# Linear attention and two MoE layers on one core: keys in groups of two token tiles, and a planner that stays with one kind of product

## The chip, the cores and the metric

One Trainium2 chip; the kernel runs on one of its NeuronCores. The metric is the device time of one execution in microseconds, as a median of several executions. TensorE (PE) multiplies, VectorE (DVE) and ScalarE (ACT) do elementwise work and reductions, GpSimd (POOL) reduces over partitions, and the queue of SyncE (SP) issues most DMA transfers. Products land in PSUM, which has eight banks; everything else that an engine reads stands in SBUF, 128 partitions wide.

## The reference

```python
# q, k, v: (4 batches, 8 heads, 576 tokens, 64), float32; w_phi: (64, 128)
def phi(x):
    proj = einsum('bhsd,df->bhsf', x, w_phi)
    proj = proj - max(abs(proj), axis=-1, keepdims=True)
    return concatenate([exp(proj), exp(-proj)], axis=-1)

q_p, k_p = phi(q), phi(k)
kv = einsum('bhsf,bhsd->bhfd', k_p, v)
z = sum(k_p, axis=2)
x = einsum('bhsf,bhfd->bhsd', q_p, kv) / (einsum('bhsf,bhf->bhs', q_p, z)[..., None] + 1e-6)
x = x.transpose(0, 2, 1, 3).reshape(2304, 512)         # tokens x (heads * 64)
h = x @ moe_w_in;  x = maximum(0.01 * h, h) @ moe_w_out      # 512 -> 2048 -> 512
h = x @ moe2_w_in; r = maximum(h, 0); out = (r * r) @ moe2_w_out
```

## The kernel before

Three stages follow each other on TensorE: the attention of batch 0; layer 1 with the attention of batches 1 to 3 put between its products; layer 2.

**Kinds of product.** A number that must keep float32 accuracy is multiplied either plain (TensorE takes such a product in two passes, which the trace shows as two records) or split into two halves that float32r holds exactly, with three float32r products in place of one (high by high, low by high, high by low). The copy that makes the high half is a CAST or an ACTIVATE, the low half a TENSOR_TENSOR on VectorE.

**Attention** (`k_pair` and `q_pair`) goes by batch and pair of heads, 16 pairs in all. The 576 keys of a head are four tiles of 128 tokens and 64 left-over tokens; the left-over tokens of both heads make a fifth tile, with a load of its own (krt). Per tile, in this order: `proj` multiplies the keys by w_phi into a PSUM bank (split from batch 1 on, but plain for the left-over tokens of all batches), `center` takes the maximum on VectorE (kmx, L1128) and negates it (L1130), `expo` runs two exponentials per head on ScalarE straight from the bank (kp, L1142), which then is free, and `kv` multiplies them by the values (vt, plain products of 65 columns) into an accumulating bank. For batches 1 to 3 a key tile can use bank 1 only, a query product bank 1 or 0, and bank 0 is also the accumulator's: two banks serve all the attention there. `q_pair` does half of the queries of a pair: product, copy out of the bank (qps), an absolute maximum over partitions on GpSimd (qm), exponentials, numerator and denominator products (with kvh, which is kv, or from batch 2 on its halves kvh and kvl), two copies per head out of the bank (qnum, qden), a reciprocal of 1.9 us on VectorE (L1321), a product, and the two halves of x, written to xr.

**Layer 1** (`moe`) goes over five blocks of tokens and 16 chunks of d_ff, 80 steps. A step of a full block is twelve products of 512 columns with xr and weights (called x products below) and twelve with gh and gl, the halves of the activation. A block can begin when the x of all its tokens is written; block 0 needs all of batch 0. **Layer 2** (`h_unit`, `y_unit`) uses products of 384 columns from xc and of 256 columns from its weights.

**SBUF.** arena, room and more hold the weights of layer 1 in slots; later arena, room, w and w_2 hold those of layer 2. Slots of arena begin at varied offsets of 32 bytes (`LINE`), and `new` pads some tiles and shifts others by 32 bytes.

**Order.** Nothing waits by hand. `Plan.add` records each operation with the engines that may run it, a cost, a position (its priority, built from the numbers in `P`) and what it reads and writes; `Plan.order` plays all engines forward and gives each the ready operation of lowest position, and the instructions are issued in that order. An operation with two possible engines (most high halves, some copies) goes to the one that takes it first. Each engine then works through its own queue in order. While TensorE has nothing in the planner's first 95 us, it is given filler products on zeros (`fill`).

Of the kernel before, what the change touches and what calls it, by code (L numbers as in the profile page):

```python
# [41 lines left out]
LINE = 16  # L42
SHIFTED = ("kvh", "kvl", "gh", "gl")
MOVED = ("gh", "gl")

P = dict(
    ring=6, wf=2, raws=3, k0=-115.69, kz=(-22.16, -25.13, -28.64), kp0=14.6, kp=22.44, ks=1.84, kvd=6.19, kb=0, pk=0, pq=0, pn=1, qk=2.73, qk2=13.5,
    q20=-8.75, qd=(3.27, -21.24, 20.79, 10.82, -2.12, -17.72, 26.78), wlead=30.91, wl0=-7.1, ydelay=16.3, xs=(174.51, 74.74, 10.17), xl=11.4, xk=4.78,
    xk2=8.22, xst=74.82, xld=24.14, lead=43.44, slead=-24.15, w2lead=29.72, ylead=53.84, evac=-12.29, stage0=-99.0, stage=14.29, stage2=-10.59,
    pl=-1.44, c_alt=43.95, sq_alt=7.93, klead=27.27, qlead=25.53, hi_alt=0.31, dve_alt=34.87, port=1.25, lat=0.28, issue=0.47, dma=2.5, rate=320e3,  # L50
    kvc=0.9, fill=95, cold=4.98, coldf=2.2,
# [29 lines left out]
class Plan:  # L81
# [31 lines left out]
    def order(self, filler=None):  # L113
        now, n_done, seq, port = 0.0, 0, 0, 0.0
# [6 lines left out]

        def make_ready(op):
            for e, (_, extra) in op.engines.items():
                heapq.heappush(ready[e], (op.pos + extra, id_of[op], op))
# [19 lines left out]
        while n_done < len(self.ops):  # L144
            for e in free:
                while free[e] <= now:
                    skipped, found = [], None
                    while ready[e]:
# [4 lines left out]
                        if can(op):  # L153
                            found = op
# [29 lines left out]
                    if e == "PE" and now < P["cold"]:  # L184
                        cost *= P["coldf"]
# [32 lines left out]
def attention_moe_moe(ctx: ExitStack, tc: tile.TileContext, qd, kd, krd, vd, wpd, wd, out):  # L218
# [30 lines left out]
    arena = ring.tile([128, NSLOT * size], F32, name="arena")  # L249
    more = first.tile([128, 2, chunk], F32, name="more")  # L250
    first.tile([128, LINE // 2], F32, name="edge")
    inside = [(k, 0) for k in range(RING - 2)] + [(k, 1) for k in range(RING)]
    slots = [[None, None] for _ in range(RING)]
    starts, words = [], 0
    for k, h in inside:
        words += LINE // 2 if h == 0 else LINE // 2 * (words // (LINE // 2) % 2)
        starts.append(words)
        slots[k][h] = arena[:, words:words + chunk]
        words += chunk
# [51 lines left out]
    def new(tag, shape, dtype, shift=0):  # L311
# [4 lines left out]
        for d in shape[1:]:  # L316
            size *= d
# [48 lines left out]
    def pe(c):  # L366
        return {"PE": (c, 0)}
# [1088 lines left out]
```

## Time and profile before

| | us |
|---|---|
| median of 3 executions | 988.54 (987.70 to 989.52) |
| profiled execution, its time | 989.24 |
| profiled execution, its span | 987.2 |
| TensorE busy in the span | 963.8 (98%) |
| VectorE busy | 784.7 (79%) |
| ScalarE busy | 562.2 (57%) |
| GpSimd busy | 90.6 (9%) |

The span runs from the first to the last instruction of the profiled execution; times within it count from its start. Layer 1 begins at 72.6 us, the attention ends at about 476 us, layer 2 begins at some 610 us. The granted clock of TensorE was 0.997 of full speed over the whole span. Matmuls are pipelined: a product's length in a row overlaps the next one's, so how long a run of products takes is read from the start of the run to the start of the next row.

### The profile page before, as it was taken

To read this page: it belongs to the slowest core of one execution; us is meant where nothing else is said; L and a number is where in the kernel's file an instruction comes from. 1 tells how busy PE (TensorE), PEld (TensorE's weight loads), DVE (VectorE), ACT (ScalarE), POOL (GpSimd) and SP (SyncE) were. 2 spreads that over 40 slices of the span, in tenths; PEclk is the share of its full clock that TensorE was granted. 3 is DMA by queue.
4 is the path that set the end of the run, shared out by engine and by line. 5 is a ranking of instruction groups with operands and counts; after the bars stand their busy time and mean duration, and the time that the engine had idled before them with its cause. 6 is when DMAs were issued, how large, how long until landed. Compare 5 with 4: busy or idle time off the path is not lost.

```text
span 987.2 us, 16603 instructions
## 1 busy us (share of the span) xinstructions
PE 963.8 (98%) x5855; PEld 859.7 (87%) x5855; DVE 784.7 (79%) x1678; ACT 562.2 (57%) x1325; POOL 90.6 (9%) x52
## 2 busy tenths in 40 slices
PE   9999999999999999999999999999999999999997
PEld 7788777878888788878888899999999999999996
DVE  6999999799999999996334421778997787888878
ACT  7988777777777887775333332343633434334342
POOL 2221011011110111010000000000000000200101
PEclk9999999999999999999999999999999999999999
DMA  7449889868988598991689489788975293918623
GB/s 268 148 170 290 293 288 317 276 240 280 313 302 292 192 319 280 330 321 64 226 304 339 171 295 333 314 341 281 301 293 207 114 361 146 275 20 306 153 76 64
DMA packets 90290, 244.37 MB, mean 248 GB/s; under 512 B 8032, under 2 KB 33504, under 8 KB 87136
## 3 DMA queue, kind: packets, MB, share of 16 engines
q1 hardware_dynamic: 86896, 239.12, 69.0%
q0 software_dynamic: 3312, 4.20, 2.9%
q8 instruction: 46, 0.75, 0.3%
q14 instruction: 36, 0.29, 0.1%
HBM read 166.48 MB, written 76.81 MB: 246 GB/s over the span
## 4 chain that ended last, share of the span: by engine, by line
PE 58%; DVE 32%; DMA 4%; issue 3%; ACT 2%; DVEq 0%; ACTq 0%; SPq 0%
PE bank L330 58%; DVE qden L1321 4%; DMA raw<-wd 3%; DVE wf L465 2%; DVE s L339 2%; DVE gl L339 2%; DVE room L339 2%; DVE kmx L1128 2%; DVE raw L460 2%; DVE g L970 1%; DVE qel L339 1%; DVE qm L339 1%; DVE qs L339 1%; DVE kmx L1130 1%; DVE qnum L1324 1%
## 5 line engine op out<-in xcount | busy, mean ns | idle before, releaser
L330 PE MATMUL bank<-gh,arena 128*128 128x512 f32 (+1 forms) x640 | 203.3, 376 | 0.0
L330 PE MATMUL bank<-xr,arena 128*128 128x512 f32 (+1 forms) x720 | 165.8, 374 | 0.0
L339 DVE TENSOR_TENSOR gl<-g,gh 128x512 fp32r<-128x512 f32 (+2 forms) x176 | 94.1, 539 | 68.6 <-ACT gh L334 68.1
L330 PEld LDWEIGHTS bank<-xr,arena 128*128 128x128 f32 x720 | 123.5, 188 | 22.2
L330 PEld LDWEIGHTS bank<-gh,arena 128*128 128x128 f32 x640 | 117.6, 189 | 20.0
L330 PE MATMUL bank<-gl,arena 128*128 128x512 f32 (+1 forms) x320 | 119.4, 373 | 0.3 <-DVE gl L339 0.3
L1251 POOL PARTITION_ALL_REDUCE qm<-qps x32 | 73.8, 2305 | 388.1 <-ACT qps L334 244.1
L334 ACT ACTIVATE gh<-g 128x512 fp32r<-128x512 f32 (+2 forms) x168 | 83.6, 502 | 36.9 <-PE bank L330 34.8
L1142 ACT ACTIVATE kp<-bank,kmx 128x128 f32<-128x128 f32 x288 | 82.3, 371 | 28.9 <-DVE kmx L1130 25.0
L625 ACT ACTIVATE g<-bank 128x512 f32<-128x512 f32 (+1 forms) x80 | 44.1, 552 | 82.0 <-PE bank L330 81.1
L330 PE MATMUL bank<-xc,w 128*128 128x384 f32 x504 | 89.8, 335 | 0.1
L330 PEld LDWEIGHTS bank<-xc,w 128*128 128x128 f32 x504 | 87.1, 188 | 0.6 <-DVE g L814 0.5
L330 PE MATMUL bank<-arena,sc 128*128 128x256 f32 x648 | 85.1, 283 | 0.1
L330 PEld LDWEIGHTS bank<-arena,sc 128*128 128x128 f32 x648 | 80.4, 188 | 1.8 <-DVE y L970 0.3
L334 ACT ACTIVATE sc<-s 128x512 fp32r<-128x512 f32 (+1 forms) x70 | 37.8, 541 | 73.8 <-DVE s L339 36.1
L330 PEld LDWEIGHTS bank<-vt,kp 128*128 128x128 f32 x576 | 71.4, 191 | 5.3 <-issue 1.5
L330 PE MATMUL bank<-vt,kp 128*128 128x65 f32 (+1 forms) x576 | 72.6, 271 | 0.6 <-ACT qnum L334 0.6
L330 PEld LDWEIGHTS bank<-gl,arena 128*128 128x128 f32 x320 | 60.5, 189 | 9.5 <-DVE gl L339 1.3
L339 DVE TENSOR_TENSOR sc<-s,sc 128x512 fp32r<-128x512 f32 (+1 forms) x96 | 51.6, 555 | 19.3 <-ACT sc L334 18.4
L814 DVE TENSOR_TENSOR g<-bank,g 128x384 f32<-128x384 f32 x72 | 40.0, 555 | 30.8 <-PE bank L330 24.9
L1321 DVE RECIPROCAL qden<-qden 128x288 f32<-128x288 f32 x32 | 62.2, 1944 | 0.8 <-ACT qden L1307 0.8
L330 PE MATMUL bank<-arena,gh 128*128 128x256 f32 x324 | 59.9, 281 | 0.0
(142 smaller groups left out, 1837.2 us busy)
## 6 DMA issues: line engine op xcount, KB each, us to landing
arena<-wsd SPq DMA_DIRECT2D x72, 512.0 KB, 5.2
raw<-wd SPq DMA_DIRECT2D x64, 512.0 KB, 5.0
xc<-xcd SPq DMA_DIRECT2D x28, 768.0 KB, 12.5
arena<-wcd SPq DMA_DIRECT2D x10, 1792.0 KB, 8.0
wsd<-arena SPq DMA_DIRECT2D x28, 512.0 KB, 5.7
wid<-room SPq DMA_DIRECT2D x24, 512.0 KB, 4.2
wcd<-room SPq DMA_DIRECT2D x24, 512.0 KB, 4.9
xcd<-xc SPq DMA_DIRECT2D x14, 768.0 KB, 10.1
```

The costliest lines, as they stand in the source:

```text
L330: nc.tensor.matmul(out=o, lhsT=lhsT, rhs=rhs, start=start, stop=stop, **kw)
L334: nc.scalar.activation(out=out, in_=in_, func=ACTF.Copy)
L339: ENG[e].tensor_tensor(out=out, in0=a, in1=b, op=ALU.subtract)
L460: nc.vector.tensor_scalar(out=low, in0=low, scalar1=29, scalar2=None, op0=ALU.logical_shift_right)
L465: nc.vector.scalar_tensor_tensor(out=t["f"].bitcast(I32), in0=high, scalar=3, in1=low, op0=ALU.logical_shift_left, op1=ALU.bitwise_or)
L625: nc.scalar.activation(out=t["g"], in_=banks[hb.bank][:, 0:N], func=ACTF.Prelu, alpha=0.01)
L814: nc.vector.tensor_tensor(out=t[o], in0=m(z), in1=t["a"], op=ALU.add)
L970: nc.vector.tensor_tensor(out=o, in0=a, in1=b, op=op)
L1128: nc.vector.tensor_reduce(out=mx[1], in_=o, axis=AX.X, op=ALU.max, apply_absolute_value=True)
L1142: nc.scalar.activation(out=u["kp"][:, s, h, :], in_=banks[pr.bank][:, h * 128:(h + 1) * 128], func=ACTF.Exp, scale=sg, bias=u["mx"][:, s, ...
L1251: nc.gpsimd.partition_all_reduce(out_ap=t["m"].rearrange("p h s -> p (h s)"), in_ap=t["ps"].rearrange("p h s -> p (h s)"), channels=128, r ...
L1321: nc.vector.reciprocal(out=t["d"], in_=t["d"])
```

## The change

What changes:

- Keys. `KGROUPS` names the groups. Batch 0 keeps five. In batches 1 to 3 the groups are left-over tokens with tile 0, tiles 1 and 2, and tile 3: 3, 4 and 2 heads' tiles with one maximum, one negation and one bank each. The left-over tokens come with the other keys in one load of 640 columns, and in batches 1 to 3 they are split with them and multiplied by the halves w2h and w2l.
- Planner. A product of layer 1 has the kind "m", all others none. If the ready product of lowest position on TensorE is of another kind than the last one, and one of the last kind is ready within `stick` = 2.0 of its position, that goes first; a change to "m" costs `switch` = 0.096 in the plan.
- Numbers. Nearly every position and several costs in `P` differ.
- Places. `LINE` shifts are gone. Slots of arena follow each other without gaps; for layer 2 the weights for y start 32 words (`STEP`) into arena, and other tiles are padded.
- Buffers. vt has one in place of two, kvh and kvl two in place of three, kmx four of another shape; kp is twice as long.
- Dead branches for `kb` are gone.
- Filler products go from 183 to 220.

```diff
-LINE = 16
-SHIFTED = ("kvh", "kvl", "gh", "gl")
-MOVED = ("gh", "gl")
+LINE = 8
+STEP = 32
+EDGE = 24
+KGROUPS = (
+    tuple(((t,), k) for k, t in enumerate((4, 0, 1, 2, 3))),
+    (((4, 0), 0), ((1, 2), 2), ((3,), 4)),
+)
...
-    ring=6, wf=2, raws=3, k0=-115.69, kz=(-22.16, -25.13, -28.64), kp0=14.6, kp=22.44, ks=1.84, kvd=6.19, kb=0, pk=0, pq=0, pn=1, qk=2.73, qk2=13.5,
+    ring=6, wf=2, raws=3, k0=-140.1, kz=(-10.15, -15.45, -39.25), kp0=13.19, kp=13.3, ks=2.06, kvd=6.19, kb=0, pk=0, pq=0, pn=1, qk=2.72, qk2=13.71,
...
+                    if e == "PE" and found and kind_of(found) != kind:
+                        rest = [i for i in ready[e] if i[2].engine is None and i[0] <= item0 + P["stick"] and kind_of(i[2]) == kind and can(i[2])]
+                        if rest:
+                            heapq.heappush(ready[e], (item0, id_of[found], found))
+                            item = min(rest)
+                            ready[e].remove(item)
+                            heapq.heapify(ready[e])
+                            found = item[2]
...
+                        if op.engines[e][2] and op.engines[e][2] != kind:
+                            cost += P["switch"]
+                        kind = op.engines[e][2]
...
-        "kt": ("a", 2), "krt": ("a", 2), "vt": ("a", 2), "kh": ("a", 1), "kl": ("a", 1), "kmx": ("a", 3), "ksb": ("a", 1),
-        "kp": ("a", 2), "kvf": ("a", 1), "kvh": ("a", 3), "kvl": ("a", 3),
+        "kt": ("a", 2), "vt": ("a", 1), "kh": ("a", 1), "kl": ("a", 1), "kmx": ("a", 3), "ksb": ("a", 1),
+        "kp": ("a", 2), "kvf": ("a", 1), "kvh": ("a", 2), "kvl": ("a", 2),
...
+    wslots = [arena[:, k * size + STEP * (k > 0):(k + 1) * size + STEP * (k > 0)] for k in range(NSLOT)] + [room, None, None, None]
+    shared = [arena[:, 0:size], arena[:, STEP:size + STEP]]
...
-        load(32768, tpos[0] - lead, get_r, w=[krt])
-        load(262144, tpos[0] - lead, get_k, w=[kt])
+        load(327680, tpos[0] - lead, get_k, w=[kt])
...
-        for n, (tt, pos) in enumerate(zip((4, 0, 1, 2, 3), tpos)):
-            m = 1 if tt == 4 else 2
+        for tiles, pos in KGROUPS[b > 0]:
+            pos = tpos[0] + P["ks"] * pos
+            heads = [(tt, h) for tt in tiles for h in range(1 if tt == 4 else 2)]
+            m = len(heads)
```

What this does to the order shows at three places. First TensorE in batch 1, between products of layer 1 (xr, gh and gl; room,kh and room,kl are split key products, vt,kp the products with the values, qs and qe query products and numerators; bank_75 and bank_76 are banks 0 and 1). Before:

```order
L330 MATMUL bank_76<-room,kh 128x256
L330 MATMUL bank_76<-room,kl 128x256
L330 MATMUL bank_76<-room,kh 128x256
L330 MATMUL bank_75<-vt,kp 128x65 x4
L330 MATMUL bank_81<-gh,arena 128x512
L330 MATMUL bank_81<-gl,arena 128x512
L330 MATMUL bank_81<-gh,arena 128x512
L330 MATMUL bank_82<-gh,arena 128x512
L330 MATMUL bank_82<-gl,arena 128x512
L330 MATMUL bank_82<-gh,arena 128x512
L330 MATMUL bank_77<-xr,arena 128x512 x6
L330 MATMUL bank_76<-room,kh 128x256
```

and in the new order:

```order
L343 MATMUL bank_76<-qs,arena 128x288 x2
L343 MATMUL bank_77<-xr,arena 128x512 x6
L343 MATMUL bank_76<-qe,kvh 128x288 x2
L343 MATMUL bank_75<-qe,kvh 128x288 x2
L343 MATMUL bank_77<-xr,arena 128x512 x6
L343 MATMUL bank_76<-room,kh 128x256
L343 MATMUL bank_76<-room,kl 128x256
L343 MATMUL bank_76<-room,kh 128x256 x2
L343 MATMUL bank_76<-room,kl 128x256
L343 MATMUL bank_76<-room,kh 128x256
L343 MATMUL bank_75<-qs,arena 128x288 x2
L343 MATMUL bank_79<-gh,arena 128x512
```

Before, one tile's three key products stand between stretches of layer 1 and the next tile's come behind twelve products of it; now two tiles' six products follow each other, and two numerators and a query product stand directly beside other attention products.

Second VectorE some 25 instructions ahead of the last write of batch 0's x (xr<-qnum and xr<-qnum,xr write x; raw<-raw, wf<-raw, arena<-wf and arena<-wf,arena shift, join, cast and split weights; qm<-qps,qm is the absolute maximum of a query product). Before:

```order
L336 CAST xr<-qnum 128x64
L339 TENSOR_TENSOR xr<-qnum,xr 128x224
L339 TENSOR_TENSOR xr<-qnum,xr 128x64
L465 SCALAR_TENSOR_TENSOR wf<-raw 128x512
L460 TENSOR_SCALAR raw<-raw 128x512
L339 TENSOR_TENSOR qm<-qps,qm 128x576
L1321 RECIPROCAL qden<-qden 128x288
L1324 TENSOR_TENSOR qnum<-qnum,qden 128x288
L1128 TENSOR_REDUCE kmx<-bank_76 128x2
L1130 TENSOR_SCALAR kmx<-kmx 128x2
L336 CAST xr<-qnum 128x32
L339 TENSOR_TENSOR xr<-qnum,xr 128x32
```

and in the new order:

```order
L473 TENSOR_SCALAR raw<-raw 128x512
L352 TENSOR_TENSOR xr<-qnum,xr 128x224
L352 TENSOR_TENSOR xr<-qnum,xr 128x64
L478 SCALAR_TENSOR_TENSOR wf<-raw 128x512
L352 TENSOR_TENSOR qm<-qps,qm 128x576
L349 CAST arena<-wf 128x512
L352 TENSOR_TENSOR arena<-wf,arena 128x512
L1143 TENSOR_REDUCE kmx<-bank_76 128x4
L1144 TENSOR_SCALAR kmx<-kmx 128x4
L1325 RECIPROCAL qden<-qden 128x288
L1328 TENSOR_TENSOR qnum<-qnum,qden 128x288
L473 TENSOR_SCALAR raw<-raw 128x512
```

Behind the same two writes of x (224 and 64 columns) the next reciprocal stood fourth; it now stands seventh, behind the cast and the split of a weight tile and a key group's maximum and negation.

Third SP's queue at the program's start (vt are values, kt keys, qt queries, raw weights). Before:

```order
L1080 DMA krt<-krd 64x128
L1076 DMA kt<-kd 128x512
L1084 DMA vt<-vd 128x650
L1212 DMA qt<-qd 128x576 x2
L1080 DMA krt<-krd 64x128
L1076 DMA kt<-kd 128x512
L1084 DMA vt<-vd 128x650
L1080 DMA krt<-krd 64x128
L444 DMA raw<-wd 128x512
L1212 DMA qt<-qd 128x576
L1076 DMA kt<-kd 128x512
```

and now:

```order
L1091 DMA kt<-kd 128x640
L1095 DMA vt<-vd 128x650
L1216 DMA qt<-qd 128x576 x2
L1091 DMA kt<-kd 128x640
L457 DMA raw<-wd 128x512 x2
L1216 DMA qt<-qd 128x576
L457 DMA raw<-wd 128x512
L1091 DMA kt<-kd 128x640
L457 DMA raw<-wd 128x512
L1216 DMA qt<-qd 128x576
L1095 DMA vt<-vd 128x650
```

The second load of values stood fourth behind the first; it now stands ninth, behind weights and queries, and waits there for TensorE's last product on the first values.

## Rows read from the trace of the kernel before

**Rows 1.** The page's busy times: engine, busy us (share of the span), instructions.
```profile
PE 963.8 (98%) x5855; PEld 859.7 (87%) x5855; DVE 784.7 (79%) x1678; ACT 562.2 (57%) x1325; POOL 90.6 (9%) x52
```

**Rows 2.** Busy time by stage: stretch, its length, PE, PEld, DVE, ACT, POOL busy.
```profile
7.70:472.00 464.30, 452.20 (x2482) 372.00 (x2481) 431.24 (x859) 359.17 (x926) 73.77 (x32) 1.00 0.77 261
30.00:72.60 42.60, 42.03 (x335) 34.09 (x333) 41.57 (x86) 38.40 (x115) 13.23 (x6) 1.00 0.47 154
135.80:438.10 302.30, 293.81 (x1549) 244.10 (x1548) 287.08 (x571) 231.51 (x577) 42.06 (x18) 0.99 0.83 287
476.60:572.00 95.40, 95.40 (x433) 78.54 (x432) 35.35 (x76) 32.76 (x61) 0.00 (x0) 1.00 0.78 276
```

**Rows 3.** TensorE's waits, 72 to 460 us: waited for, total, times, longest.
```profile
PE bank L330 <- ACT kp L1142: 4.1, 6, 1.6
PE bank L330 <- ACT qps L334: 2.5, 4, 1.4
PE bank L330 <- DVE kvh L336: 2.0, 1, 2.0
```

**Rows 4.** Timeline of TensorE at 107 us: start, length, instruction, [idle before, releaser].
```profile
106.98 0.38 PE L330 MATMUL bank<-room,kh 128*128 128x256 f32 x1 [1.58 <-ACT kp L1142]
```

**Rows 5.** Timeline of VectorE ahead of that place.
```profile
103.26 1.95 DVE L1321 RECIPROCAL qden<-qden 128x288 f32<-128x288 f32 x1
105.12 0.36 DVE L1128 TENSOR_REDUCE kmx<-bank 128x2 f32<-128x256 f32 x1
```

**Rows 6.** TensorE's groups of layer 2's h products: count, busy us, mean ns.
```profile
L330 PE MATMUL bank<-xc,w 128*128 128x384 f32 x504 | 89.8, 335 | 0.1
...
L330 PE MATMUL bank<-xc,room 128*128 128x384 f32 x252 | 45.9, 339 | 0.0
...
L330 PE MATMUL bank<-xc,arena 128*128 128x384 f32 x252 | 45.3, 338 | 0.0
```

**Rows 7.** Timeline of TensorE in layer 1 alone.
```profile
515.31 2.96 PE L330 MATMUL bank<-xr,arena 128*128 128x512 f32 x12
...
518.10 0.40 PE L330 MATMUL bank<-gh,arena 128*128 128x512 f32 x1
...
520.88 2.88 PE L330 MATMUL bank<-xr,arena 128*128 128x512 f32 x12
523.60 0.39 PE L330 MATMUL bank<-gh,arena 128*128 128x512 f32 x1
```

**Rows 8.** Timeline of VectorE at 220 us.
```profile
219.77 1.10 DVE L336 CAST kvh<-kvf 128x512 fp32r<-128x512 f32 x1
```

**Rows 9.** Timeline of TensorE, a product of left-over tokens.
```profile
56.98 0.48 PE L330 MATMUL bank<-wst,krt 64*128 64x128 f32 x2
57.40 1.46 PE L330 MATMUL bank<-zeros 128*128 128x128 bf16 x23
```

**Rows 10.** Timeline of TensorE behind a run of plain products.
```profile
102.38 0.48 PE L330 MATMUL bank<-gh,arena 128*128 128x512 f32 x1
102.70 0.39 PE L330 MATMUL bank<-gl,arena 128*128 128x512 f32 x1
102.93 0.62 PE L330 MATMUL bank<-gh,arena 128*128 128x512 f32 x2
```

**Rows 11.** Timeline of VectorE ahead of layer 1.
```profile
66.11 0.69 DVE L465 SCALAR_TENSOR_TENSOR wf<-raw 128x512 int32<-128x512 int32 x1
66.71 0.42 DVE L460 TENSOR_SCALAR raw<-raw 128x512 int32<-128x512 int32 x1
67.05 0.42 DVE L336 CAST arena<-wf 128x512 fp32r<-128x512 f32 x1
```

**Rows 12.** DMA issues: count, KB each, median us to landing.
```profile
vt<-vd SPq DMA_DIRECT2D x16, 325.0 KB, 4.2
```

More of the change, by code (lines that the diff above doesn't have):

```diff
@@ L113, in order @@
     def order(self, filler=None):
-        now, n_done, seq, port = 0.0, 0, 0, 0.0
+        now, n_done, seq, port, kind = 0.0, 0, 0, 0.0, None
         events, order = [], []
@@ L248, in attention_moe_moe @@
     NSLOT = 3
-    arena = ring.tile([128, NSLOT * size], F32, name="arena")
+    arena = ring.tile([128, NSLOT * size + 4 * STEP], F32, name="arena")
     more = first.tile([128, 2, chunk], F32, name="more")
-    first.tile([128, LINE // 2], F32, name="edge")
+    first.tile([128, EDGE], F32, name="edge")
     inside = [(k, 0) for k in range(RING - 2)] + [(k, 1) for k in range(RING)]
     slots = [[None, None] for _ in range(RING)]
[L254 to L259, printed above, removed]
-    words += LINE // 2 * (words // (LINE // 2) % 2)
+    for n, (k, h) in enumerate(inside):
+        slots[k][h] = arena[:, n * chunk:(n + 1) * chunk]
     for k in range(2):
@@ L307, in right, with new @@
             wslots[NSLOT + 3] = p.tile([128, size], F32, name="w_2")
[L308 removed]
+            p.tile([128, 3 * STEP], F32, name="gap")
         return pools["r"]
[L311 removed]
+    def new(tag, shape, dtype):
         pl, n = tags[tag]
         where = late() if pl == "b" else right() if pl == "r" else pools[pl]
[L314 to L324 removed]
+        if tag == "kmx":
+            return where.tile([128, LINE], dtype, tag=tag, name=tag, bufs=n + 1)[:, 0:8].rearrange("p (a b c) -> p a b c", a=2, b=4)
+        if tag == "vt":
+            return where.tile([128, 656], dtype, tag=tag, name=tag, bufs=n)
+        if tag == "qel":
+            flat = where.tile([128, 4 * HALF + STEP], dtype, tag=tag, name=tag, bufs=n)[:, 0:4 * HALF]
+            return flat.rearrange("p (a b c) -> p a b c", a=2, b=2)
+        if tag == "pt":
+            return where.tile([128, 2 * QD + EDGE], dtype, tag=tag, name=tag, bufs=n)[:, 0:2 * QD]
         return where.tile(shape, dtype, tag=tag, name=tag, bufs=n)
@@ L563, in take, with at_slot @@
         return [under_val[tag] for tag in under.get(k, ())]
+    def at_slot(kind, k):
+        return shared[kind == "y"] if k == SHARED else wslots[k]
     def w2_load(n, pos):
@@ L1135, in expo @@
-            def expo(e, m=m, pr=pr, u=u):
-                u["kp"] = new("kp", [128, 2, 2, 128], F32)
-                for s, sg in ((0, 1.0), (1, -1.0)):
-                    if not bias:
-                        nc.scalar.activation(out=u["kp"][:, s, 0:m, :], in_=u["sb"], func=ACTF.Exp, scale=sg)
-                        continue
-                    for h in range(m):
+                nc.vector.tensor_scalar(out=mx[0], in0=mx[1], scalar1=-1.0, scalar2=None, op0=ALU.mult)
+            def expo(e, m=m, pr=pr, u=u):
+                u["kp"] = new("kp", [128, 2, 4, 128], F32)
+                for h in range(m):
+                    for s, sg in ((0, 1.0), (1, -1.0)):
@@ L1161, in k_pair @@
[L1161 to L1168 removed]
+            cost = sum((0.415 if plain else 0.25) if tt == 4 else 0.536 if plain else 0.36 for tt in tiles)
@@ L1169, in k_pair @@
+            plan.add(pe(cost), pos, proj, r=[wsv, kt] if plain else [wcv, *ksrc], w=[pr])
+            plan.add({"DVE": (m * 128 * 1.04e-3 + 0.25, 0)}, pos + 0.4, center, r=[pr], w=[mx]).shared = False
+            plan.add({"ACT": (0.5 * m, 0)}, pos + 0.8, expo, r=[pr, mx], w=[kp])
+            plan.add(pe(P["kvc"] * m), pos + P["kvd"] + P["ks"] * (len(tiles) - 1), kv, r=[kp, vt], w=[acc])
         pos = tpos[-1] + P["kvd"] + 0.1
```

145 lines of the change are left out of this document (62 added, 83 removed).

## The prediction

> **What bounds the kernel now.** I read the page's busy times first, then the busy time by stage, then the waits of TensorE, and last the timeline at single places. TensorE (PE) is busy 963.8 of 987.2 us and VectorE (DVE) 784.7 [rows 1]; a gain has to come out of TensorE's own time or its few waits. By stage: ahead of layer 1 (30 to 72.6 us) VectorE is busy 41.57 of 42.6 us, and the next stage waits for its last x. From 135.8 to 438.1 us, where the attention of batches 1 to 3 runs between products of layer 1, both are nearly full: TensorE 293.8, VectorE 287.1 of 302.3 us (95.0%). From 476.6 to 572 us layer 1 runs alone and TensorE has no idle time at all [rows 2]; layer 2 is alike. So there are three sorts of time to move: the length of a product, TensorE's waits inside the attention, and the start.
>
> The waits have one pattern. Between 72 and 460 us TensorE waits 4.1 us for the exponentials of a key group (kp), 2.5 us for a query copy (qps), 2.0 us once for kvh [rows 3]. At 106.98 us it sat idle 1.58 us before a key product [rows 4]: the group before still held bank 1, its maximum (kmx) began on VectorE at 105.12 us only, behind a reciprocal of 1.95 us [rows 5], and its exponentials (kp), which follow the maximum on ScalarE, are what TensorE was released by. Each key group passes PE, VectorE and ScalarE queues once, in one bank; each is one more chance of such a wait.
>
> **Part 1: places in SBUF.** The words of the change don't name it, but the diff moves nearly every tile. In the built program I compared, product by product, the address that TensorE streams from with that of the weights it loads meanwhile, both modulo 256 bytes. Before, they are equal for the xc products whose weights stand in w and 128 bytes apart for those in room and arena: 335 ns against 339 and 338 [rows 6]. In layer 1, with nothing else going on, twelve xr products whose weights in arena stand at unequal places take 515.31 to 518.10 us, 2.79 us; the next twelve, with weights at equal places of the same tile, take 520.88 to 523.60 us, 2.72 us; the twelve of gh and gl between them, at mixed places, take 2.78 us [rows 7]. After, all products of 384 and 512 columns stand at equal places, those of y (256 columns) 128 bytes apart. The sum: some 39 of the 64 twelves of xr are unequal now, times 0.07 is 2.7 us, and I take 2.5; 64 twelves of gh and gl by 0 to 0.06 us, 0 to 3.8 us, and I take 1.0, as many of them are equal now; xc 504 by 3.5 ns, 1.8 us, of which I take 1.5, since durations overlap; y 1,512 products: no row has this place, so 0 to 1.2% (the share of [rows 6]) of half a 512-column product (115 ns), 0 to 2.1 us, and I take 1.5. Together **-6.5 us**, bounds -2.5 and -10. It lies on TensorE's path, which nothing covers.
>
> A rule speaks against this. The Trainium skill, "SBUF — State Buffer", section "Who interferes with whom", says that TensorE has two independent read ports, one for the moving operand and one for the weights, and that it never waits on anyone; by it this part would give 0 and the sum below would come to 988.4. The products compared in [rows 6, 7] differ by the place and disagree; that the place isn't what tells them apart is the second rival.
>
> **Part 2: key groups.** Five groups of a pair become three in batches 1 to 3 (60 become 36). VectorE loses 24 maxima and 24 negations; but the splits of the keys grow from 512 to 640 columns, and the planner puts 14 more copies on VectorE (174 to 188 in all), which gives most of it back. None of it is on TensorE's path by itself: 0. What counts is the bank. Counted in the order, a bank that a query copy must clear is asked for again after only six layer-1 products (six twelfths of 2.79 us, 1.4 us [rows 7]) in 30 of 47 places before and in 11 of 46 after; key uses of a bank fall from 57 to 34. If waits go with these counts, kp loses 4.1 x 23/57 = 1.7 us and qps 2.5 x 19/30 = 1.6 us [rows 3]. Against it, casts of kvf on VectorE rise from one to four; the one in the trace took 1.10 us [rows 8], and TensorE's 2.0 us wait hung on it. With 0.8 us for that the counts say -2.5 us. What is late next is VectorE, which the new order fills further (first rival, +8 us); I take **-0.5 us**, nearer the counts, bounds -6 and +8.
>
> **Part 3: left-over tokens.** In 12 pairs one plain product (two passes, 56.98 to 57.40 us, 0.42 us [rows 9]) becomes three fp32r products of 128 columns. No row has one. From below a quarter of a 512-column product each (2.72/12/4 = 0.057, three 0.17 us); from above, if each takes as long as one of those passes, 0.63 us. Per pair -0.25 to +0.21 us; I take -0.08, nearer the middle, so **-1.0 us**, bounds -3 and +2.5.
>
> **Part 4: one kind for longer.** Between the first and the last x product, the runs of layer-1 products that attention interrupts fall from 122 to 86, and changes from plain fp32 to fp32r over the whole program from 70 to 42. After one, the first gh product lasts to 102.70, 0.32 us, the next 0.23 [rows 10]. 28 x 0.09 = **-2.5 us**, bounds 0 and -3.3: not every change in the trace shows it.
>
> **Part 5: the start.** Layer 1 begins when batch 0's last x is written, and VectorE sets that. In the new order VectorE has, ahead of that write, two more weight splits, three more weight casts, a weight join, a shift and three more numerator copies, less one query copy and two casts of x. By the time from one such instruction's start to the next one's, 0.60 us for a join and some 0.34 for a shift or a cast [rows 11], that is +3.9 us. TensorE meanwhile does 1.2 us of batch 1's products that came later before; the rest of its wait is filler products (220, before 183), which delay nothing that is ready. **+2.7 us**, bounds +1 and +5. Values (vt) have one buffer instead of two: SP issues a load only when the last product on the old values is done, and it lands 4.2 us later [rows 12]. In batch 0 some 4.2 to 5.3 us of other products stand in between, so up to 1 us may be missing three times, in a stretch that VectorE sets anyway; from batch 1 on the shortest distance is 8.6 us. Behind that waiting load on SP stand weight loads, which are issued tens of us ahead. I take +0.5 us, bounds 0 and +6. Loads of krt vanish, off the path. Layer 2 has the same order on TensorE and SP; only part 1 touches it.
>
> **The sum.** -6.5 - 0.5 - 1.0 - 2.5 + 2.7 + 0.5 = -7.3 us. The profiled execution took 989.24 us (span 987.2 and 2.0 around it), 0.7 above the median 988.54. 989.2 - 7.3 = 981.9: **982 us**.
>
> **Rivals.** (1) VectorE becomes the bound: slower. The planner pulls the attention forward: its last product stands on TensorE behind 564 x products before and behind 516 in the new order, four steps of layer 1 (a step is two twelves, 5.5 us [rows 7]) or 22 us of TensorE's time earlier, while VectorE's instructions ahead of it, each at its duration in the trace, sum to 3 us less only. That product lies just ahead of 472 us now. So VectorE must do between 7.7 and some 446 us, 438 us, what it does now up to 472 us, 431 us of busy time [rows 2] less 3; some 10 us of that are ends of instructions that overlap the next one once it never idles. That needs 96 to 98%; it holds 95.0% from 135.8 to 438.1 us and 97.6% ahead of layer 1 [rows 2]. At 95%, 418 to 428 us of work take 440 to 450 us, 2 to 12 us more than there are; with 8 us in place of my -0.5 the time is 990 us. For it: the queue is in order, and weight staging stands between urgent steps. Against it: the x of each batch is then ready two to four steps ahead of the block that needs it, so lateness hurts only where an attention product waits. It decides from a busy share of 96%. (2) The places give nothing: 981.9 + 6.5 = 988.4 us. For it: the difference is 1 to 2%, and the slots of arena take turns in one order. Against: it shows in two stages, and in layer 1 within one tile. (3) The grouping doesn't do what it says: the waits only move to other operations in the same two banks, and the changes of kind cost nothing. 981.9 + 0.5 + 2.5 = 985 us. For it: numerators have the same counts as before (25 of 47 places below 2.5 us in both).
>
> **How the numbers follow.** Forecast 0.50, rival 1 0.18, rival 2 0.09, rival 3 0.17, other mishaps of a new order 0.06. A measurement can tell about 0.2%, 2 us, from no change: below 986.6 is faster, above 990.5 slower. The forecast's own range is 975 to 986, its terms' bounds taken half at once; rivals 2 and 3 lie close to it, and rival 1 has its middle at 990. **971 to 992** leaves out the far half of rival 1 and the mishaps, some 0.17. Faster: the forecast and rival 3, 0.67. Slower: half of rival 1, the mishaps and some of the forecast's edge, 0.18. Same: rival 2 and the near part of rival 1, 0.15.
>
> **What would show it.** Part 1: twelves of xr at 2.72 us throughout 476 to 572 us, and room, arena and w of xc at one duration, 335. If they stay at 2.79 and 339, rival 2. Part 2: TensorE's waits for kp and qps at half of theirs now. Part 4: fewer first products of 0.32 us. Part 5: the first xr product at 75 to 76 us (72.6 now); at 79 or later vt or VectorE is worse than I think. Rival 1: VectorE above 97% from 136 to 440 us with TensorE's waits there doubled. The forecast is wrong if TensorE's time from 476 us on isn't some 4 us shorter, or if attention ends later, counted from layer 1's start, than TensorE's own work explains.

## The result, and the profile after

| | kernel before | changed kernel |
|---|---|---|
| median of executions | 989.03 us | 996.51 us (995.12 to 998.34) |
| ratio to before | | 1.0077 (95%: 1.0060 to 1.0093) |
| span of the profiled execution | 987.2 | 995.3 |
| layer 1 begins | 72.6 | 76.9 |
| from there to the 577th x product (the attention lies in this stretch) | 404.1 | 408.6 |
| TensorE's waits in that stretch | 11.5 | 15.8 |
| from there to the 913th x product (layer 1 alone) | 123.7 | 121.4 |
| from there to the last product | 380.2 | 381.9 |

The change makes the kernel slower by 0.8%, where 982 us had been forecast. Of the 8.1 us between the spans, 4.3 are the later start and 4.5 the attention; the rest of the program is 0.7 shorter (some y products stand ahead of the 913th x product in one kernel and behind it in the other, so the last two lines of the table are read together).

First the busy times of the page, as in [rows 1]:

```profile
PE 968.1 (97%) x5904; PEld 865.7 (87%) x5904; DVE 788.2 (79%) x1643; ACT 557.1 (56%) x1313; POOL 91.1 (9%) x52
```

VectorE (DVE) has 35 instructions fewer and 3.5 us more work. By stage, with the columns of [rows 2] (ahead of layer 1; from its start to the last numerator; the middle of the attention; layer 1 alone):

```profile
30.00:76.90 46.90, 46.68 (x384) 38.19 (x384) 44.98 (x98) 40.22 (x126) 13.56 (x6) 1.00 0.50 156
76.90:458.40 381.50, 365.74 (x1928) 304.20 (x1928) 367.82 (x683) 286.75 (x720) 54.03 (x23) 0.99 0.82 278
144.20:463.70 319.50, 307.89 (x1626) 257.37 (x1625) 306.62 (x575) 238.55 (x597) 44.53 (x19) 0.99 0.80 276
485.40:580.80 95.40, 95.40 (x439) 79.69 (x439) 36.97 (x77) 35.05 (x63) 0.00 (x0) 1.00 0.68 230
```

In the middle of the attention VectorE is busy 306.62 of 319.5 us, 96.0% (95.0% before). TensorE's waits there, as in [rows 3] (72 to 490 us):

```profile
PE bank L343 <- ACT kp L1150: 6.3, 9, 1.5
PE bank L343 <- ACT qps L347: 2.4, 4, 1.4
PE bank L343 <- ACT qnum L347: 2.1, 4, 0.9
PE bank L343 <- ACT qden L1311: 1.7, 2, 1.2
PE bank L343 <- DVE qs L352: 1.6, 1, 1.6
PE bank L343 <- DVE gl L352: 1.4, 1, 1.4
```

The wait for kp, which the groups were to halve, went from 4.1 to 6.3 us. One of them shows how a group waits. Timeline of all engines (start, length, instruction, idle before; rows of other work left out):

```profile
205.38 0.68 DVE L478 SCALAR_TENSOR_TENSOR wf<-raw 128x512 int32<-128x512 int32 x1
205.78 2.47 POOL L1255 PARTITION_ALL_REDUCE qm<-qps  x1 [28.94 <-ACT qps L347]
205.99 1.52 DVE L473 TENSOR_SCALAR raw<-raw 128x512 int32<-128x512 int32 x1
207.43 0.68 DVE L1143 TENSOR_REDUCE kmx<-bank 128x4 f32<-128x512 f32 x1
208.14 0.17 DVE L1144 TENSOR_SCALAR kmx<-kmx 128x4 f32<-128x4 f32 x1
...
208.34 2.17 ACT L1150 ACTIVATE kp<-bank,kmx 128x128 f32<-128x128 f32 x8 [2.08 <-DVE kmx L1144]
...
210.57 0.38 PE L343 MATMUL bank<-room,kh 128*128 128x256 f32 x1 [1.47 <-ACT kp L1150]
```

The group's products began at 203.84 us and were done by 205. VectorE had a weight join and a weight shift, 2 us, ahead of their maximum; ScalarE sat idle 2.08 us for it, then needed 2.17 us for eight exponentials in a row, and only then was the bank free. A group is one wait instead of two, but its chain in one bank is longer, and it hangs on VectorE's queue as before.

The weight shift took 1.52 us here, where most take 0.42, and GpSimd's maximum (the POOL row) ran beside it. Of VectorE's 111 shifts and casts of 512 columns ten take 0.7 us or more (seven of 103 before), every one beside such a maximum, 8.0 us (6.1) beyond their usual length together. That is 1.9 of VectorE's 3.5 us more work. Nine others beside a maximum stayed short, and no run changes this alone.

What follows on TensorE's clock (the column after POOL's busy time is the granted clock):

```profile
209.00:211.50 2.50, 1.03 (x9) 0.94 (x9) 2.40 (x5) 2.50 (x9) 0.00 (x0) 1.00 0.31 121
211.50:218.50 7.00, 7.00 (x25) 5.94 (x25) 6.86 (x16) 5.58 (x15) 0.00 (x0) 0.52 0.74 240
```

After two waits of 1.38 and 1.47 us within 7 us the granted clock was 0.52 for 7 us, the lower of its two levels (1.2 GHz), and 3.4 us of full speed were lost: more than the two waits. The kernel before has one such fall, half as long, behind its 2.0 us wait for kvh [rows 3]:

```profile
222.80:226.30 3.50, 3.50 (x12) 2.46 (x10) 3.44 (x6) 2.34 (x5) 0.00 (x0) 0.52 0.89 279
```

So of the attention's +4.5 us, 4.3 are waits, 1.7 are clock, and 0.8 are the left-over tokens (below); shorter layer-1 products and fewer changes of kind give some of it back. The split belongs to these two executions: of the changed kernel's four, the slowest (998.34 us) has a granted clock of 0.993 over its span and the fastest (995.12 us) 0.997.

### The profile page after: what moved, and what is told of

The parts are those of the page before. It is cut to its first block, busy times and chain, and to the rows that moved or that the text cites. A ratio compares the mean times of both kernels' runs of the same rounds, so it can differ in the third digit from the quotient of the medians.

```text
span 995.3 us, 16625 instructions
## 1 busy us (share of the span) xinstructions
PE 968.1 (97%) x5904; PEld 865.7 (87%) x5904; DVE 788.2 (79%) x1643; ACT 557.1 (56%) x1313; POOL 91.1 (9%) x52
## 4 chain that ended last, share of the span: by engine, by line
PE 55%; DVE 34%; issue 4%; DMA 4%; ACT 3%; SPq 0%; DVEq 0%; ACTq 0%
PE bank L343 55%; DVE qden L1325 4%; DVE gl L352 3%; DVE wf L478 2%; DVE s L352 2%; DVE qs L352 2%; DMA raw<-wd 2%; DVE room L352 2%; DVE kmx L1143 2%; DVE raw L473 2%; DVE qel L352 1%; DVE g L986 1%; DVE qm L352 1%; ACT kp L1150 1%; DVE xr L352 1%
## 5 line engine op out<-in xcount | busy, mean ns | idle before, releaser
L343 PE MATMUL bank<-gh,arena 128*128 128x512 f32 (+1 forms) x640 | 201.0, 375 | 0.0
L343 PE MATMUL bank<-xr,arena 128*128 128x512 f32 (+1 forms) x720 | 162.9, 371 | 0.0
L347 ACT ACTIVATE gh<-g 128x512 fp32r<-128x512 f32 (+2 forms) x162 | 79.8, 498 | 35.6 <-PE bank L343 32.4
L1150 ACT ACTIVATE kp<-bank,kmx 128x128 f32<-128x128 f32 x288 | 79.9, 377 | 24.0 <-DVE kmx L1144 17.7
```

What stands on the lines that cost most here:

```text
L343: nc.tensor.matmul(out=o, lhsT=lhsT, rhs=rhs, start=start, stop=stop, **kw)
L347: nc.scalar.activation(out=out, in_=in_, func=ACTF.Copy)
L1150: nc.scalar.activation(out=u["kp"][:, s, h, :], in_=banks[pr.bank][:, h * 128:(h + 1) * 128], func=ACTF.Exp, scale=sg, bias=u["mx"][:, s, ...
```

## The experiments

All medians stand beside runs of the kernel before on the same chip (988.9 to 990.3 us), so some 1.5 us between runs beside different medians tell nothing. Where an order is said to be the same, every instruction of every engine stands where it stood.

**Places.** The slots of layer 1's weights in arena are moved by 32 bytes (w2h and w2l, which stand behind them, by 128):

```diff
-        slots[k][h] = arena[:, n * chunk:(n + 1) * chunk]
+        slots[k][h] = arena[:, n * chunk + 8:(n + 1) * chunk + 8]
```

> The changed kernel in its own order, instruction for instruction, with the slots of layer 1's weights in arena moved by 32 bytes, so that all xr, gh and gl products that use them stand 32 bytes apart from their weights instead of at equal places. Theory (the place decides how long a 512-column product takes, 227 ns at equal places against some 232): about 1,340 products of 512 columns by 4.5 to 6 ns, less 0.5 us for block 4's 256-column products, +5.5 to +7.5 us, 1002 to 1004 us; twelve xr products in layer 1 alone go from 2.72 back to 2.79 us. Rival (the place is not what tells the products apart): 996.5 us, twelves stay at 2.72.

Measured 998.94 us, 1.0094 (1.0070 to 1.0117) of before, against 1.0077 (1.0060 to 1.0093) for the changed kernel: 2.4 us more by the medians, within the noise, and less than the 1002 us expected. In layer 1 alone, first the changed kernel, then this one:

```profile
523.53 2.88 PE L343 MATMUL bank<-xr,arena 128*128 128x512 f32 x12
526.25 0.39 PE L343 MATMUL bank<-gh,arena 128*128 128x512 f32 x1
```

```profile
521.51 2.96 PE L343 MATMUL bank<-xr,arena 128*128 128x512 f32 x12
524.31 0.40 PE L343 MATMUL bank<-gh,arena 128*128 128x512 f32 x1
```

Twelve products take 2.72 and 2.80 us; nothing but the place differs. The starts of all records give 227 and 233 ns a product, 6.7 us more over the whole, of which the profiled execution, the slowest of four, shows 4.6: in the attention part of it only shortens waits. The rival falls, by the rows and not by the time. So does, for this case, the rule of the Trainium skill, "SBUF — State Buffer", section "Who interferes with whom", that the two read ports of TensorE are independent and it never waits on anyone; by it these two rows would be alike, and the measurement decides.

The y weights moved by another 32 bytes:

```diff
-STEP = 32
+STEP = 40
```

> The changed kernel in its own order, with layer 2's y weights in arena moved by another 32 bytes: 1,134 of the y products (256 columns) stand 96 bytes from their activations instead of 128. Theory (for 256 columns places half a 256-byte row apart, or equal, are the slow ones, 119 to 120 ns against 117.5): -1.1 to -2 us, 994.5 to 995.4 us, and the intervals of y's products in the trace fall from 119 to 117.5 ns. Rival (the prediction's: half apart or equal is as good or better for 256 columns): 996.5 us or up to 2 us more.

Measured 997.04 us. Layer 2's y products, the changed kernel and this one:

```profile
L343 PE MATMUL bank<-arena,sc 128*128 128x256 f32 x648 | 85.3, 284 | 0.1
```

```profile
L343 PE MATMUL bank<-arena,sc 128*128 128x256 f32 x648 | 85.4, 283 | 0.1
```

No gain in the time. From start to start the y products are 119 ns apart at 128 bytes and 118 at 96 (medians; 118 before, at 32 and 96): under 1 ns, and the prediction's place of 128 bytes isn't the better one.

The kernel before in its own order, with places alone changed:

```diff
-        slots[k][h] = arena[:, words:words + chunk]
+        slots[k][h] = arena[:, n * chunk + 64:(n + 1) * chunk + 64]
...
-SHIFTED = ("kvh", "kvl", "gh", "gl")
+SHIFTED = ("kvh", "kvl")
```

> The kernel before, instruction for instruction in its order, with places alone changed: products of 512 and 384 columns at equal places, y's 32 to 64 bytes apart. The 32-byte test of the changed kernel gave 227 against 233 ns for 512 columns, but only half of the time in the attention came through. Theory: some 1,080 products by 3.5 ns is 3.8 us of TensorE's time, of which 1.2 in layer 1 alone and 0.7 in layer 2 come through whole and half of 2.6 in the attention: -3 us, 986 to 987.5 us. Rival (VectorE's pace takes all that lies in the attention): -1.5 us, 988.5.

Measured 987.67 us, 0.9984 (0.9968 to 0.9999). It lies between the theory and the rival. (In another version a y slot overlapped its neighbour by 64 bytes; it took 1043 us and tells nothing of places.) Layer 1 alone went from 123.7 to 122.8 us, layer 2 stayed at 380.2, and in the attention (404.1 to 402.7) the gain is no more than the fall of the clock that this execution doesn't have; its waits are 1.5 us longer. In this order places are worth 1.3 us by the medians, 0.1 to 3.2 by the interval, not 6.5.

**VectorE.** The reciprocal is cut from 288 columns to 32, in either kernel and its own order, and the copy of the denominators ahead of it writes a constant, so the quotient is left out:

```diff
-            nc.vector.reciprocal(out=t["d"], in_=t["d"])
+            nc.vector.reciprocal(out=t["d"][:, 0:32], in_=t["d"][:, 0:32])
```

> The changed kernel in its own order, but every reciprocal of 288 columns (1.95 us on VectorE) does 32 columns, and the denominators are a constant, so the output is not the reference's: 32 times some 1.6 us, 51 us of VectorE's time, is left out. Theory (VectorE sets both the start of layer 1 and the attention's waits): layer 1 starts at 66 to 70 us instead of 76.9, TensorE's waits between there and the last attention product fall from 15.8 to under 7 us, 977 to 982 us. Rival (waits come from the order of banks on TensorE and ScalarE, not from VectorE): the start moves, but 12 to 16 us of waits stay, 986 to 991 us.

> The kernel before in its own order with the same shortened reciprocals (32 of 288 columns, a constant denominator, 51 us of VectorE's time left out; the output is not the reference's). Theory (both kernels are paced by VectorE in the attention, the changed one more): the kernel before loses less than the 17 us that the changed one lost; 976 to 981 us, TensorE's waits between layer 1's start and the last attention product fall from 11.5 to some 4 us, and the changed kernel without that load (979.6) is level with it within 2 us. Rival (the changed kernel's extra time is not VectorE's doing): before falls by 15 to 17 us as well, to 972 to 974, and stays 6 or more ahead.

Measured 979.60 us (changed) and 976.93 us (before). The waits of TensorE that are left, changed kernel first:

```profile
PE bank L343 <- ACT kp L1150: 2.8, 3, 1.5
PE bank L343 <- DVE qs L352: 1.6, 1, 1.6
PE bank L343 <- DVE gl L352: 1.1, 1, 1.1
PE bank L343 <- ACT qnum L347: 0.5, 2, 0.3
```

```profile
PE bank L330 <- ACT kp L1142: 1.8, 2, 1.3
PE bank L330 <- ACT qps L334: 1.5, 3, 0.6
PE bank L330 <- ACT qden L1307: 1.0, 2, 0.5
PE bank L330 <- ACT qnum L334: 0.3, 1, 0.3
```

The waits in the attention fall from 15.8 to 6.2 us and from 11.5 to 5.0, and no fall of the clock is left in the attention. Although the rows name ScalarE nearly throughout, most of these waits were VectorE's doing. Without that load the attention takes 390.9 us in the changed kernel and 391.7 before: its loss there is gone, and the 2.7 us between the medians are the start (75.7 against 72.8), which hardly moved. What was expected of the start was wrong: with VectorE relieved of 8 us and more ahead of it (busy 57.0 in place of 64.8 us, 50.3 in place of 59.2 before), TensorE has no wait from 28 us to the start, and its own queue of products and fillers holds the start where it was. So 2.9 of the 4.3 us by which the changed kernel starts later stand in TensorE's queue as well.

**Fillers.**

```diff
-        mm(banks[4][:, 0:FILL], zeros, zeros, False, False, skip_group_check=True)
+        mm(banks[4][:, 0:FILL // 2], zeros, zeros[:, 0:FILL // 2], False, False, skip_group_check=True)
```

> The changed kernel in its own order with filler products of 64 instead of 128 columns: 220 fillers ahead of and around layer 1's start take less. With shortened reciprocals the start of layer 1 had stayed at 75.7 us, with TensorE waiting for nothing. Theory A (the fillers themselves keep TensorE's queue full, so the start follows them): layer 1 starts at 72 to 74.5 us and the whole is 2 to 4 us shorter. Theory B (the prediction's: fillers delay nothing, VectorE's work sets the start): 76 to 77 us, and 996 to 997 us. If the clock falls where products get fewer, the start is later than 77.

Measured 1008.97 us, layer 1 from 87.3 us. The reason lies in the first 30 us. The same query products, changed kernel first:

```profile
9.95 0.75 PE L343 MATMUL bank<-qt,wst 64*128 64x288 f32 x2
10.62 0.70 PE L343 MATMUL bank<-wst,kt 128*128 128x256 f32 x2
```

```profile
11.25 1.33 PE L343 MATMUL bank<-qt,wst 64*128 64x288 f32 x2
12.51 0.79 PE L343 MATMUL bank<-wst,kt 128*128 128x256 f32 x1
```

1.26 instead of 0.67 us from start to start (the last view ends after one product): until some 30 us every product runs at half pace, and then no longer. In front of them stood 36 fillers of 53 ns instead of 107, and a wait of 1.2 us for the first keys. From the end of batch 0's first numerators (20.76 and 30.85 us) both kernels take 56 us to layer 1, though 184 of the fillers, half as long now, lie there. TensorE waits for VectorE and ScalarE there instead (2.5 us in four waits), and a fall of the clock costs 1.7 us. So with VectorE at its full load the later fillers delay next to nothing, as theory B has it, though its times (996 to 997 us) were missed. That the first ones carry the pace is argued: all were shortened at once.

**The rule on kinds.** Without it (with stick at 0 its condition is switched off), and with each of its two numbers alone:

```diff
-    kvc=0.405, switch=0.096, stick=2.0, fill=95, cold=4.98, coldf=2.2,
+    kvc=0.405, switch=0.0, stick=0.0, fill=95, cold=4.98, coldf=2.2,
```

> The changed kernel without the planner's rule on kinds (both numbers at zero): layer 1's products are interrupted 96 times instead of 86 (122 before). Theory (the rule is worth its changes of kind, 10 by 0.09 us, and leaves the waits alone): 996.5 to 998 us, with TensorE's waits in the attention at 14 to 17 us. Rival (the rule holds attention work back that VectorE and ScalarE then get late): 990 to 993 us, waits at 9 to 12.

> The changed kernel with the holding-back of the other kind off (stick 0), but the plan's price for a change to layer 1 kept (switch 0.096). Counted in its order, the last numerator stands behind 516 x products (as in the changed kernel; 540 without the whole rule, which took 980.9 us); VectorE's instructions ahead of it sum to 418.2 us and TensorE's to 417.9 (415.7 and 420.7 in the changed kernel; 411.7 and 429.0 without the rule). Theory (the price in the plan makes layer 1 look slower than it is, so the attention is pulled so far forward that VectorE sets its pace): the last numerator comes some 42 us after VectorE's sum, at 460 us with 3 us less of TensorE's work done, 999 to 1003 us. Rival (staying with one kind is what costs, by holding back urgent attention products): 980 to 984 us.

> The changed kernel with the holding-back kept (stick 2.0) and the plan's price for a change at zero. In its order the last numerator stands behind 540 x products, VectorE's instructions ahead of it sum to 414.3 us and TensorE's to 423.5. Theory (VectorE's work against TensorE's ahead of that product decides): last numerator at 454 to 457 us, 990 to 993 us, between the changed kernel and the one without the rule. Rival (staying with one kind is what costs): 995 to 998 us, as the changed kernel. If neither part costs alone: 981 us.

Measured 980.85 us without the rule (0.9919 of before, 0.9900 to 0.9937), 994.54 with the price alone, 990.8 with the holding-back alone. Without the rule the start is the same (76.9 us), the attention takes 392.7 us in place of 408.6, its waits 7.3 in place of 15.8, and the clock does not fall:

```profile
PE bank L343 <- ACT kp L1150: 2.3, 4, 0.8
PE bank L343 <- ACT qnum L347: 1.4, 2, 1.1
PE bank L343 <- ACT qden L1311: 1.0, 3, 0.5
PE bank L343 <- DVE qps L349: 0.7, 1, 0.7
```

This looked like the cause, but 980.9 is 9 us below the lower of the two expectations. The sums of VectorE's and TensorE's work ahead of the last numerator put the holding-back right (990 to 993 expected), and the price alone at least 4.5 us too high and on the wrong side of the changed kernel.

**Groups and numbers.** Without the rule, groups undone (`KGROUPS` with five single groups in all batches), and without the rule with the numbers of before:

> The changed kernel without the kind rule and with key groups of single token tiles in all batches (left-over tokens still split, one load): grouping undone. In its order the last numerator stands behind 576 x products, VectorE's sum ahead of it is 429.7 us and TensorE's 453.1. Theory (groups save bank waits for the exponentials and VectorE's small reductions): TensorE's waits rise from 7.3 to 10 to 14 us, mostly kp, and the time from 980.9 to 984 to 988 us. Rival (groups give nothing, as waits only move to other operations of the same banks): 980 to 982 us.

> The changed kernel with the positions and costs of before (the price of values per head 0.45) and without the kind rule: groups, split left-over tokens, places and the single values buffer alone. In its order the last numerator stands behind 552 x products, VectorE's sum ahead of it is 422.2 us and TensorE's 437.9. Theory (the ratio of these sums decides, 0.964 here against 0.960 without the rule and 0.988 in the changed kernel): 981 to 987 us, and layer 1's start earlier than 76.9 us, since the new positions put more of the next batch ahead of it. Rival (the new numbers carry the gain): 987 to 992 us.

Measured 994.12 and 987.39 us. Single groups cost 13 us, about twice the theory's upper end, but 5.4 us of it is one wait for kp, and the longest fall of the clock of all runs (17 us, 8.5 us lost) begins in it: together more than the whole, so nothing of it is shown to be the groups' own. With the old numbers the attention takes 393.7 us, as with the new ones (392.7); in this pair the new numbers only bring layer 1's start from 81.3 to 76.9 us (it had been expected ahead of 76.9).

**Nudges.** By now each new order had brought its own surprise. Two numbers of the plan were moved by 4 and 7 per cent, which means nothing by itself, in three kernels (in the kernel before kvc goes from 0.9 to 0.935):

```diff
-    kvc=0.405
+    kvc=0.42
```

```diff
-lat=0.28
+lat=0.3
```

> The changed kernel without the kind rule (980.9 us), and one cost of the plan moved by 4% (kvc 0.405 to 0.42), a nudge that means nothing by itself but gives another order. Theory R (the kind rule is what costs): 979 to 985 us. Rival L (an order of this planner is a draw, and the run without the rule was a lucky one): anywhere from 981 to 997 us, above 988 as likely as below. By the sums ahead of the last numerator (VectorE 411.7, TensorE 426.9, ratio 0.964) 982 to 985.

> The changed kernel without the kind rule, the plan's latency 0.30 in place of 0.28. Theory R: 979 to 986 us. Rival L: anywhere from 981 to 997 us. By the sums ahead of the last numerator (VectorE 413.3, TensorE 425.5, ratio 0.971) 985 to 989.

> The changed kernel with its kind rule, and the same nudge (kvc 0.405 to 0.42). Theory R: 990 to 1000 us, as the changed kernel (996.5) and its two halves (990.8, 994.5). Rival L: anywhere from 981 to 997 us. By the sums ahead of the last numerator (VectorE 418.0, TensorE 433.9, ratio 0.963) 982 to 985.

> The changed kernel with its kind rule, the plan's latency 0.30 in place of 0.28. Theory R: 990 to 1000 us. Rival L: anywhere from 981 to 997 us. By the sums ahead of the last numerator (VectorE 412.9, TensorE 425.5, ratio 0.970) 985 to 989.

> The kernel before, with the same plan cost of the values products moved by 4% (kvc 0.9 to 0.935) and nothing else: another order of the same work. Theory S (the order of the kernel before is a chosen one among draws, so that any change of the plan gives most of that up): 993 to 1002 us, with layer 1's start some us later than 72.6 or TensorE's waits in the attention above 15 us. Rival T (orders of the kernel before lie close together, and the new kernel's spread of 981 to 997 is its own): 987 to 991 us.

> The kernel before, with the plan's latency 0.30 in place of 0.28 and nothing else. Theory S: 993 to 1002 us. Rival T: 987 to 991 us.

| median, us (layer 1 begins) | as it is | kvc nudged | lat nudged |
|---|---|---|---|
| before | 989.0 (72.6) | 985.5 (76.0) | 989.7 (78.2) |
| changed, without the rule | 980.9 (76.9) | 986.6 (81.9) | 993.4 (78.8) |
| changed | 996.5 (76.9) | 992.3 (81.5) | 991.0 (78.8) |

Orders of the same attention and layers lie up to 12.6 us apart. The rule costs 15.7, 5.7 and -2.4 us by the three pairs: it is not shown to cost, and the 980.9 is a good draw as much as a better kernel. The 993.4 again has a fall of the clock, around a wait of 7.38 us for gl (granted clock in the second row, in the column after POOL):

```profile
445.77 0.79 PE L343 MATMUL bank<-gl,arena 128*128 128x512 f32 x1 [7.38 <-DVE gl L352]
```

```profile
440.00:450.00 10.00, 4.23 (x10) 3.36 (x11) 8.75 (x16) 5.78 (x13) 0.00 (x0) 0.51 0.46 186
```

That wait and the 5.1 us lost in the fall are more than the 10.3 us between its span and that of the kernel without the rule: here, as with the single groups, one event makes the difference.

The nudged orders aren't pure draws: each has 261 to 282 fillers (183 before, 220 changed), and each starts layer 1 later than its kernel as it is, by 1.9 to 5.6 us. So the two starts, at least, look chosen. In time the kernel before isn't a chosen low draw: its nudges are no slower (985.5, below both expectations, and 989.7). By the means of the three rows, 988.1, 987.0 and 993.3 us, everything but the rule is worth about 1 us, and with the rule the change loses 5; with three draws a row, neither is settled. The sums ahead of the last numerator, my third forecast, were too low in all four, by 1.6 to 7.3 us (982 to 985 for a_j1, measured 992.3): they don't predict an order either.

## Why the prediction was wrong, point by point

The steps that failed are the term for TensorE's waits in the attention (part 2) and the size of the term for places (part 1). As the runs have them, the terms are -1.3 (places, in the order of before), +6.0 (waits 4.3, clock 1.7), +0.8, -2.4 and +4.3, together +7.4 where -7.3 had been forecast; the spans differ by 8.1.

- **What bounds the kernel.** Half right. The prediction saw TensorE and VectorE both nearly full in the attention, but looked for the gain in TensorE's own time and left VectorE to rival 1, with 0.18. VectorE paces the attention in both kernels, and that is shown: cutting 32 of its instructions short is worth 17 and 12 us.
- **Part 1, places, -6.5.** The mechanism was right and its size wrong. The place decides (227 against 233 ns), so rival 2 falls. In the kernel before it is worth 1.3 us by the medians. Three steps of the sum failed: y gains nothing (-1.5 taken; 118 ns from start to start before, 119 after); xc's rows fell as forecast (339 to 336 and 338 to 335 ns), but layer 2's stretch only by some 0.6 us; and "It lies on TensorE's path, which nothing covers" is wrong in the attention, where VectorE's pace takes a part of it back.
- **Part 2, groups, -0.5.** Here most of the forecast was lost. Counting how soon a bank is asked for again said -2.5 us; TensorE's waits rose by 4.3, those for kp to 1.5 times, and those for qps stayed [rows 3]. Such counts take no account of when VectorE gets to a group's maximum. The groups by themselves aren't shown to be at fault: without the rule on kinds the same groups have 7.3 us of waits, 4.2 fewer than before. Rival 1 named VectorE; its +8 us for this term was near the 6.0 measured, waits and clock together, and its weight of 0.18 looks too small. Its two tests disagree: it was to decide from a busy share of 96%, and elsewhere from 97% with twice the waits. Measured were 96.2% from 136 to 440 us and 1.4 times the waits. The 0.8 us against the counts came from a cast of kvf of 1.10 us [rows 8], one of the long ones beside GpSimd's maximum; the four in the changed kernel take 0.42. What rival 1 left out is the second price of a wait:
- **The clock,** in no term of the sum. Behind some waits of 1.5 to 2 us TensorE runs at half its clock for 3.5 or 7 us, which costs 1.7 or 3.4 us more. The trace of before had one such fall, behind the 2.0 us wait of [rows 3]. With 3.1 us at half clock behind the program's last products it makes the granted clock of 0.997 over the whole span; I read that as full speed.
- **Part 3, left-over tokens, -1.0.** Within its bounds, with the wrong sign. Three products take 0.48 us against 0.42 [rows 9], +0.8 us by all starts in the stretch. They start 0.11 to 0.20 us apart, not the 0.057 of a quarter product:

```profile
79.75 0.32 PE L343 MATMUL bank<-arena,kh 64*128 64x128 f32 x1
79.92 0.27 PE L343 MATMUL bank<-arena,kl 64*128 64x128 f32 x1
80.03 0.27 PE L343 MATMUL bank<-arena,kh 64*128 64x128 f32 x1
80.23 0.39 PE L343 MATMUL bank<-room,kh 128*128 128x256 f32 x1
```

- **Part 4, one kind for longer, -2.5.** Right, for the product itself: behind a plain product (values, numerators) the first float32r product still takes some 85 to 105 ns longer to the next start [rows 10], in nearly every place. By all starts this sums to 7.2 us before and 4.8 after: -2.4 us. What the rule does to the order was in no term: the three pairs have it between +15.7 and -2.4 us.
- **Part 5, the start, +3.2 with vt.** The right size: +4.3 us, inside the bounds, and in part by luck. VectorE's busy time from 7.7 us to the start is 5.6 us more (59.2 to 64.8) in place of 3.9. But "VectorE sets that" and "fillers ... delay nothing that is ready" are half of it: with VectorE relieved the start came 1.2 us earlier in the changed kernel and not at all in the one before, as TensorE's queue, fillers included, is about as long. No product waited for vt there.
- **Range and chances.** 971 to 992 took the terms for independent of the order. The three orders of a row lie up to 3 us (before, changed) or 6 us (without the rule) from their mean, on top of the terms' bounds. By my judgement the range should have reached to some 997, and "slower" was worth three in ten rather than two.

What stays open: whether grouping by itself is worth anything of the 13 us of one pair of orders, whether the rule on kinds costs anything, and why one order has more waits than another. The fastest kernel is the change without the rule, 980.85 us, ahead of both; its nudges, at 986.6 and 993.4, say that its lead belongs to that order.

## What to carry to other kernels

Where a planner sets the order, a change to it is a new draw: move a meaningless number twice, in the kernel before and after, and see how far the times scatter before a gain or loss is put down to the change. A transfer of work between engines and a wait are priced at the engine that paces the stage, which is found by making one of its instructions short in a fixed order; the engine that the waits name can be another. Changes that leave the order alone, like places in memory, can be read product by product from the trace, to a few ns (their time over the whole stayed uncertain by 1.5 us or more here), so test those by themselves.

## What the runs showed of the hardware

- A product of 512 columns takes 227 ns from start to start if what it streams stands at the same place modulo 256 bytes as the weights loaded meanwhile, 233 if 32 bytes apart, in one and the same order. For the 256-column products of layer 1's last block it is the other way about: xr and gh take 120 ns at equal places and 117 when 32 bytes apart (medians of the same two runs).
- Waits of 1.4 to 2 us are sometimes followed by a granted clock near 0.5, in stretches of 3.5 or 7 us, and sometimes by nothing (the 1.58 us of [rows 4], the 1.55 us at 98 us of the changed kernel). Even the same two waits in the same order differ: 1.38 and 1.47 us had 6.8 us at half clock behind them, 1.59 and 1.47 us (y weights moved) 3.4 us, and 1.76 and 1.49 us (short fillers) none. What tells them apart wasn't tried.
- With 36 short products ahead of the program in place of long ones, TensorE ran at half pace to about 30 us, while the granted clock of the profile stood at 1.00 there. The trace's first record of the clock begins at 29.95 us there (6.96 us in the changed kernel), and the column shows 1.00 where there is none: half pace at the start is seen only in the products' own durations.
